# Chunked attention and a gated MLP on one core: the startup's loads and conversions in another order, half of the v loads on a second queue

## The chip, the core and the metric

The kernel runs on one core of a Trainium2 chip. The core has five engines with an instruction stream each: TensorE (PE in the profile), VectorE (DVE), ScalarE (ACT), GpSimd (POOL) and SyncE (SP, which only issues loads and stores here). An engine takes its instructions in order; what depends on another engine or on a load waits for a semaphore. The metric is the device time of one execution in microseconds, lower is better.

## The reference

Chunked attention over 4 batches, 8 heads, 768 positions and 64 channels, followed by a gated MLP (the code here leaves out the sizes and the plain loops):

```python
for c in range(nc):                      # 24 chunks of 32 queries
    k_ctx = k[:, :, max(0, 32*c - 16):min(S, 32*c + 40)]
    v_ctx = v[:, :, max(0, 32*c - 16):min(S, 32*c + 40)]
    k_full = concat(mem_k, k_ctx); v_full = concat(mem_v, v_ctx)     # 8 memory rows ahead
    a = softmax(scale * q_c @ k_full.T)
    out[:, :, c] = a @ v_full
x = out as (4, 768, 512)
h = relu(x @ w_in)                       # 512 -> 1024
u, v = halves of h
v_n = (v - mean(v)) / sqrt(var(v) + 1e-6)
v_s = w_spatial @ v_n + b_spatial        # over the 768 positions of a batch
result = (u * v_s) @ w_out               # 512 -> 512
```

All inputs are float32 but for w_in and w_out, which arrive as 64-bit floats.

## The kernel before, in words

**Attention.** A unit is four chunks, 128 queries, of all eight heads; a batch has six units (`UB`), a group of three units shares its loads of q and k (`GU`). For unit i TensorE makes the scores (`burst`, tile `sx`), VectorE takes the maximum and subtracts it, ScalarE takes the exp (`softmax`, tile `p`), TensorE transposes p (`flip`, tile `pt`), ScalarE copies that out (`pT`), TensorE multiplies with v (`f<-vmain,pT` in the first units, `sx<-v,pT` later), VectorE divides by the sum (`xs`), TensorE transposes (`xt`), ScalarE and VectorE write x as a high part and a low part. Unit i's product with v stands behind unit i+1's scores. With `PSUMS = 3` the sums of p of the first three units are made by TensorE (`f<-halves,pT`), later ones by VectorE (`den`).

**MLP.** Every product of the MLP is three products of the tile's high and low parts: high by high, low by high, high by low (`group`, lines 748 to 750, tile `f`, four buffers). I call three such products on one slice of 128 channels a chunk. `ffn_v` makes 128 rows of v in four chunks of 128x512, `ffn_u` u in four chunks of 128x384, `spatial` the product with w_spatial, `ffn_o` the last product.

**Weights.** w_in arrives as pairs of 32-bit words. `from_f64` loads a part (128 rows, the u half or the v half of the columns), and makes of it `win_h` and `win_l`: ScalarE scales the high words, VectorE shifts and sets the sign (two instructions, lines 922 and 923), ScalarE scales the low words ("rest"), GpSimd adds them, ScalarE casts the sum to the high part, GpSimd subtracts for the low part. w_spatial (`w_sp_part`) is cast and subtracted in the same way. All these loads share four buffers (`big`).

**v and the memory rows.** A unit's v has for two halves of the heads (r = 0, 1) 32 partitions of its own rows and 24 of the next chunk (the halo), and 8 of mem_v. In batch 0 the halo is copied on the chip (`shift_v`, line 486, on ScalarE or GpSimd), and mem_v is loaded for one chunk and spread by copies (`load_mem`, `copy_mem`, line 316).

**What sets the order.** All work is recorded by `op` in a plan (class `Plan`), with a rank, a length, what it reads and what it writes; `order` is a list scheduler that writes every engine's order out from that, and the program keeps to it. The table `FIRST` says which loads of batch 0 come in which order, with ranks for w_in's conversions. `heat` adds TensorE products of which nothing is used, as many as `HOT` says. Loads go out in SP's queue, except for mem_k and the first memory rows, which go out in ScalarE's; a load waits until at most 2 MB (`AHEAD`) are under way. Eight semaphores (DMAHW0 to DMAHW7) are given to the loads in turn as the program lists them; a load waits until the load eight places earlier has landed.

Of the kernel before, what the change touches and what calls it, by code (L numbers as in the profile page):

```python
# [25 lines left out]
FIRST = [("qk", 0, (0, 0), 1), ("mem", 0, "ACT", True), ("qk", 0, (1, 2), 2), ("w", 1, 1, 40.0, 3.0),  # L26
# [4 lines left out]
LANES = 8  # L31
CLOCK0 = 1.2
SHORT = 3.4133
HOT = (7, 4, 3, 7, 7, 0, 0)
# [3 lines left out]
PSUB = 0  # L38
XLOW = 0
PSUMS = 3  # L40
VACT = 6
VNORM = {"DVE": 0.6}
VLOW = {"DVE": 0.85}
KEYS = {"ACT": 0.42, "POOL": 0.43}
WLOW = {"POOL": 1.35}
SHIFT = {"POOL": 1.08, "ACT": 0.95}
SPREAD = {"ACT": 2.6, "POOL": 3.0}


# [27 lines left out]
class Plan:  # L77
# [12 lines left out]
    def op(self, eng, us, fn, r=(), w=(), rank=0.0, moves=0.0, tail=0.0, after=None, count=0):  # L90
        n = len(self.ops)
        deps, begun = set(), set()
# [18 lines left out]
        self.ops.append((eng, us, fn, deps, rank, moves, tail, held, begun, count))  # L111
        return n

    def order(self):
# [8 lines left out]
        free = {e: 0.75 if e in ("SP", "ACT") else 0.0 for e in ENGINES}  # L123
# [10 lines left out]
        while len(out) < len(ops):  # L134
            best = None
            for e, ns in waiting.items():
                pick = None
                for n in ns:
# [14 lines left out]
                    late = max(t, free[e])  # L153
                    if any(max(free[x], t) + y < late + either[n][e] for x, y in either[n].items() if x != e):
                        continue
                    c = (late, ops[n][4], n)
                    if pick is None or c < pick:
                        pick = c
# [3 lines left out]
            _, _, _, _, _, moves, tail, held, _, count = ops[n]  # L162
            us = either[n][e]
            if count:
                k, heat = clock.of(t), 0.5 if count in (128, 256) else 1.0
# [15 lines left out]
            free[e] = t + us  # L181
            if moves:
# [22 lines left out]
def tile_chunked_attention_gmlp(  # L205
# [67 lines left out]
    v2 = early.tile([P, T, GU * UC, D], F32, name="v2")  # L273
    ps = {name: pool(f"ps_{name}", bufs=sizes[name], space=PSUM) for name in ("f", "sx", "pt", "xt")}
# [3 lines left out]
    wsp_h = const.tile([P, ST, S], F32R, name="wsp_h")  # L278
    wsp_l3 = const.tile([P, ST - 3, S], F32R, name="wsp_l3")
# [20 lines left out]

    def heat(n, r=()):
        def go():
            if ("xt", "warm") not in t_:
                alloc("xt", "warm", [P, 512], F32, psum=True)
            for _ in range(n):
                nc.tensor.matmul(t_["xt", "warm"], minus, minus.unsqueeze(1).broadcast_to([P, T, P]), start=True, stop=True, skip_group_check=True)  # L306
        if n:
            op("PE", 0.233 * n, go, r=r, w=[("xt", "warm")], rank=99.0, tail=0.25, count=2 * n)

    def clear():  # L310
        for r in range(2):
            nc.vector.memset(vmain[r * D + CH:(r + 1) * D, :, 0], 0.0)
    op("DVE", 0.2, clear, w=["clear"], rank=-1.0)
# [7 lines left out]
    line, sent, held = {}, [], {}  # L321

    def load(dst, src_, w, rank, r=(), eng="SP", rows=P, us=0.45):
# [13 lines left out]
        def go():  # L337
            me["ins"] = e.dma_start(out=dst() if callable(dst) else dst, in_=src_).ins  # L338
            if before:
# [4 lines left out]
        speed *= {P: 1.0, CH: 0.75}.get(rows, 0.4)  # L344
        n = op(eng, us, go, r=[*r, *([("load", before["n"])] if before else [])], w=[*w, ("load", len(plan.ops))],
               rank=rank, moves=n / 1e6 / speed, after=line.get(eng))
        line[eng] = me["n"] = n
# [18 lines left out]

    def early_keys():
        return [key for key in plan.writer if isinstance(key, tuple) and key[0] == "early"]

    def wsp_l(s):  # L370
        return late("wsp_l0")[:, s] if s < 3 else wsp_l3[:, s - 3]
# [19 lines left out]
    def load_qk(g, units=(0, GU - 1), pieces=1):  # L391
        i = GU * g
        b, c0 = i // UB, (i % UB) * UC
# [585 lines left out]
    for i in range(UB):  # L979
        shift_v(i)  # L980
# [79 lines left out]
```

## Time and profile before

| What | Value |
|---|---|
| median of 3 runs | 398.62 us (397.97 to 399.00) |
| the profiled execution's own time | 398.16 us |
| its span, first to last instruction | 396.1 us |
| mean granted TensorE clock | 0.983 |
| TensorE busy | 383.8 us, 97% of the span |
| VectorE, ScalarE, GpSimd busy | 49%, 42%, 28% |

The profile is one execution. A row of the chain of waits is a start, a length and what ran or was waited for; a row of the timeline is a start, a length, the engine, the line, the operation, its tiles and shapes. A row of the stretches gives a window, its length, the busy time of PE, PEld (weight loads), DVE, ACT and POOL with the number of instructions, the granted TensorE clock, the mean share of the DMA engines that was busy and the GB/s moved. "SPq" and "ACTq" are the issue of loads, "issue" is time in which an engine waited for nothing that the profile shows. Line numbers are those of the kernel before.

### The profile page before, as it was taken

Reading aid. Unit: us, or ns where it says so; the run is one execution under the profiler, and the core shown is the slowest. Engines: PE = TensorE matmul, PEld = TensorE weight load, DVE = VectorE, ACT = ScalarE, POOL = GpSimd, SP = SyncE. Lnnn points to the kernel's source line nnn. Section 1 sums busy time; section 2 is a strip of 40 time slices with the busy share of each in tenths; the row PEclk is TensorE's granted clock in tenths of the full one; section 3 lists DMA queues with packets and bytes.
Section 4 is the critical chain, followed back from the end, with each engine's and each line's share of the span. In section 5 each row is a group of like instructions: output and inputs, shape, how many; then the busy total and the mean of one; then the engine's idle time right before and its main releaser. Section 6 shows DMA issues by size and latency. Waiting matters only on the chain.

```text
span 396.1 us, 11126 instructions
## 1 busy us (share of the span) xinstructions
PE 383.8 (97%) x4864; PEld 344.3 (87%) x4864; DVE 195.7 (49%) x392; ACT 165.1 (42%) x289; POOL 110.3 (28%) x119
## 2 busy tenths in 40 slices
PE   6797999999999999999999999999999999999996
PEld 4586898999899889889988988889989889899995
DVE  2746987895546447494662315383423233514040
ACT  6686986872524235344323223343221223321212
POOL 6497686285102101010220312010222210104031
PEclk9868999999999999999999999999999999999999
DMA  7999337972165582023746010000001010000202
GB/s 249 263 289 300 120 101 159 280 211 76 43 217 79 133 267 73 2 62 121 164 134 233 1 75 7 0 3 2 2 36 46 26 55 0 0 2 0 81 1 79
DMA packets 29216, 39.53 MB, mean 100 GB/s; under 512 B 5360, under 2 KB 23280, under 8 KB 29168
## 3 DMA queue, kind: packets, MB, share of 16 engines
q1 hardware_dynamic: 28864, 38.73, 32.7%
q8 instruction: 38, 0.62, 0.7%
q10 hardware_dynamic: 304, 0.10, 0.1%
q14 instruction: 10, 0.08, 0.1%
HBM read 32.52 MB, written 6.29 MB: 98 GB/s over the span
## 4 chain that ended last, share of the span: by engine, by line
PE 91%; DMA 7%; issue 1%; POOL 1%; SPq 0%; ACT 0%; POOLq 0%
PE f L748 26%; PE f L749 25%; PE f L750 25%; PE sx L546 8%; DMA vmain<-in_v_dram 3%; PE xt L699 3%; PE pt L682 3%; DMA big<-in_moe_w_in_dram 1%; PE f L546 1%; DMA k<-in_k_dram 1%; DMA vmain<-in_mem_v_dram 1%; PE xt L306 1%; POOL vmain L486 1%; SPq L338 0%; ACT st L890 0%
## 5 line engine op out<-in xcount | busy, mean ns | idle before, releaser
L858 POOL TENSOR_TENSOR st<-st,u 128x384 f32<-128x384 f32 x32 | 33.8, 1057 | 139.3 <-DVE st L854 106.0
L748 PE MATMUL f<-wsp_h,vn 128*128 128x384 f32 x192 | 66.4, 346 | 0.0
L749 PE MATMUL f<-wsp_h,vn 128*128 128x384 f32 x192 | 65.0, 339 | 0.0
L750 PE MATMUL f<-wsp_l,vn 128*128 128x384 f32 x192 | 64.5, 336 | 0.0
L786 POOL TENSOR_TENSOR rstd<-ve,mhalf 128x1 f32<-128x1 f32 x24 | 16.6, 691 | 102.2 <-DVE ve L782 102.2
L748 PE MATMUL f<-x,win_h 128*128 128x384 f32 x128 | 44.7, 350 | 0.0
L861 ACT CAST big<-st 128x384 fp32r<-128x384 f32 x32 | 16.4, 512 | 65.1 <-POOL st L858 65.1
L749 PE MATMUL f<-x,win_l 128*128 128x384 f32 x128 | 43.3, 338 | 0.0
L750 PE MATMUL f<-x,win_h 128*128 128x384 f32 x128 | 43.2, 337 | 0.0
L854 DVE TENSOR_TENSOR st<-f,bias 128x384 f32<-128x384 f32 x32 | 17.8, 556 | 51.3 <-PE f L750 51.3
L748 PE MATMUL f<-win_h,x 128*128 128x512 f32 x96 | 39.7, 413 | 0.0
L748 PE MATMUL f<-wout,big 128*128 128x512 f32 (+1 forms) x100 | 39.0, 390 | 0.0
L749 PE MATMUL f<-wout,big 128*128 128x512 f32 (+1 forms) x100 | 38.3, 383 | 0.0
L750 PE MATMUL f<-wout,big 128*128 128x512 f32 (+1 forms) x100 | 38.2, 382 | 0.0
L750 PE MATMUL f<-win_l,x 128*128 128x512 f32 x96 | 38.1, 397 | 0.0
L749 PE MATMUL f<-win_h,x 128*128 128x512 f32 x96 | 38.0, 396 | 0.0
L748 PEld LDWEIGHTS f<-wsp_h,vn 128*128 128x128 f32 x192 | 36.0, 188 | 1.4
L749 PEld LDWEIGHTS f<-wsp_h,vn 128*128 128x128 f32 x192 | 36.1, 188 | 0.8
L750 PEld LDWEIGHTS f<-wsp_l,vn 128*128 128x128 f32 x192 | 36.1, 188 | 0.0
L778 DVE BATCH_NORM_STATS2 stats<-st 128x6 f32<-128x512 f32 x24 | 16.6, 690 | 31.6 <-ACT st L774 31.6
L865 DVE TENSOR_TENSOR big<-st,big 128x384 fp32r<-128x384 f32 x32 | 20.6, 645 | 21.9 <-ACT big L861 21.6
L890 ACT COPY st<-f 128x512 f32<-128x512 f32 (+1 forms) x25 | 14.2, 571 | 31.3 <-PE f L750 30.9
(85 smaller groups left out, 704.8 us busy)
## 6 DMA issues: line engine op xcount, KB each, us to landing
out_dram<-st SPq DMA_DIRECT2D x23, 256.0 KB
k<-in_k_dram SPq DMA_DIRECT2D x7, 800.0 KB
q<-in_q_dram SPq DMA_DIRECT2D x7, 768.0 KB
vmain<-in_v_dram SPq DMA_DIRECT2D x36, 128.0 KB
big<-in_moe_w_in_dram SPq DMA_DIRECT2D x8, 512.0 KB
vmain<-in_v_dram SPq DMA_DIRECT2D x35, 96.0 KB
big<-in_moe_w_spatial_dram SPq DMA_DIRECT2D x6, 384.0 KB
big<-in_moe_w_out_dram SPq DMA_DIRECT2D x4, 512.0 KB
```

Of the source, the lines that this page charges most:

```text
L546: nc.tensor.matmul(o, w_, m, start=start, stop=True, skip_group_check=True)
L682: nc.tensor.transpose(a[:, t], p[:, t], ident)
L748: nc.tensor.matmul(o, lh, rh, start=(j == 0), stop=False)
L749: nc.tensor.matmul(o, ll, rh, start=False, stop=False)
L750: nc.tensor.matmul(o, lh, rl, start=False, stop=(j == len(pairs) - 1))
L778: nc.vector.bn_stats(stats, t_["st", s])
L786: nc.gpsimd.tensor_tensor(a, t_["ve", i], mhalf, op=ALU.pow)
L854: nc.vector.tensor_tensor(alloc("st", s_, [P, HT], F32), t_["f", n], bias[:, tok], op=ALU.add)
L858: nc.gpsimd.tensor_tensor(a, a, t_["u", i], op=ALU.mult)
L861: nc.scalar.copy(t_["g", i][:, 0, 0:HT], t_["st", s_])
L865: nc.vector.tensor_tensor(a[:, 1, 0:HT], t_["st", s_], a[:, 0, 0:HT].bitcast(F32), op=ALU.subtract)
L890: nc.scalar.copy(alloc("st", s_, [P, N], F32), t_["f", n])
```

## The change

- **v and mem_v in batch 0.** The r = 1 half of v goes out in ScalarE's queue (`TWO = 1`, `behind`). Unit 0 has its halo loaded, too; the others' is still copied. mem_v is no longer spread: `first_mem` loads it for three units at a time, eight loads of `8x12x64`, the first set in ScalarE's queue, the second in SP's. `copy_mem` and the clearing of v's rows go.
- **w_in.** The high part is cast from the high words alone, before the low words are added; the low part is the full sum less that. Scale and cast may run on GpSimd, the subtraction on VectorE.
- **u's half of w_in** is loaded into and converted in tiles of its own (`stage_w`, `stage_z`) in the place that w_spatial's parts take later; w_spatial's casts wait for the last low part of w_in.
- **Scores** of the first units use the two halves of one `sx` tile in turn (`HALVES`), so that the next scores need not wait for the last maximum and subtraction. The sums of p are all VectorE's (`PSUMS = 0`), and the addition of the small constant moves to ScalarE. The heating products go (`HOT = ()`).
- **The order.** The list scheduler counts a VectorE operation of a marked kind and any GpSimd operation as exclusive (`port`), has other lengths, and a table `ORDER` that adds to the ranks of some 75 operations, delays their choice, or fixes their engine.

Three places in which the order moves, for engines that wait or are waited for there. First ScalarE's order around unit 2's exp. Before (the first row is unit 2's exp, `pT` the copy of its transposed p, `x<-xt` x's high part, `k_158` the keys of units 3 to 5):

```order
L654 ACTIVATE p<-p 128x512 [waits DVE_49]
L931 CAST win_h<-st 128x512 [waits Pool_49]
L913 ACTIVATE st<-big 128x512
L316 COPY k_158<-k_158 128x16x24 [waits DMAHW5_49]
L705 CAST x<-xt 128x4x128 [waits PE_49]
L685 COPY pT<-pt 128x512 [waits PE_49,Activation_49]
L913 ACTIVATE st<-big 128x512 [waits DMAHW0_49,Pool_49]
```

And now, the same stretch with buffer numbers (`p_384` is unit 2's exp, `pT_460` its copy, `v2_94` the v of units 3 to 5, `x_361` the x of units 0 to 2):

```order
L981 ACTIVATE st_423<-big_356 128x512 [waits DMAHW2_49]
L987 ACTIVATE big_356<-big_356 128x512
L695 ACTIVATE p_384<-p_384 128x512 [waits DVE_49,Activation_49]
L375 DMA v2_94<-in_v_dram 32x4x768 [waits DMAHW4_49]
L353 CAST win_h_112<-st_423 128x512 [waits DVE_49]
L353 CAST win_h_112<-stage_z_99 128x512 [waits DVE_49]
L733 COPY pT_460<-pt_440 128x512 [waits PE_49,Activation_49]
L353 COPY k1_374<-k1_374 128x16x24
L704 ACTIVATE den_453<-den_453,tiny_119 128x8 [waits DVE_49]
L981 ACTIVATE stage_z_99<-stage_w_98 128x512 [waits DMAHW5_49]
L987 ACTIVATE stage_w_98<-stage_w_98 128x512
L538 COPY v2_94<-v2_94 24x4x192 [waits DMAHW6_49]
```

A load of v, with its wait for a semaphore of the loads, now stands between unit 2's exp and the copy of its transposed p.

Second, SP's order of loads from the second k on. Before (`big` takes parts of w_in):

```order
L338 DMA k1_158<-in_k_dram 128x4x400 [waits DMAHW3_49]
L338 DMA v2_94<-in_mem_v_dram 8x4x64 [waits DMAHW6_49]
L338 DMA v2_94<-in_mem_v_dram 8x4x64
L338 DMA big_410<-in_moe_w_in_dram 128x1024 [waits DMAHW4_49,DMAHW0_49,Pool_49]
L338 DMA big_554<-in_moe_w_in_dram 128x1024 [waits DMAHW1_49,Activation_49,Pool_49]
L338 DMA v2_94<-in_v_dram 32x4x256 [waits DMAHW5_49,DMAHW2_49]
```

And now (`stage_w` takes the u half of w_in):

```order
L375 DMA k1_374<-in_k_dram 128x4x400 [waits DMAHW4_49,DMAHW2_49]
L375 DMA stage_w_98<-in_moe_w_in_dram 128x1024 [waits DMAHW3_49]
L375 DMA v2_94<-in_v_dram 32x4x768 [waits DMAHW6_49]
L375 DMA v2_94<-in_v_dram 24x4x64
L375 DMA stage_w_98<-in_moe_w_in_dram 128x1024 [waits DMAHW4_49,DMAHW0_49]
L375 DMA v2_94<-in_mem_v_dram 8x12x64 [waits DMAHW1_49]
L375 DMA v2_94<-in_mem_v_dram 8x12x64 x3
L375 DMA v2_94<-in_mem_v_dram 8x12x64 [waits DMAHW5_49]
```

The eight loads of mem_v now stand behind the last part of w_in; in turn they take DMAHW1, 2, 3, 4 and on.

Third, TensorE's order around its first MLP products. Before (`sx<-k_158` are the scores of unit 3; a row `x32` is 32 instructions):

```order
L682 MATMUL pt<-ident,p 128x128 x4
L546 MATMUL sx<-k_158,q_297 32x64 x32
L546 MATMUL f<-halves,pT 128x2 x4
L546 MATMUL f<-vmain,pT 32x64 x32
L748 MATMUL f<-win_h,x 128x512
L749 MATMUL f<-win_h,x 128x512
L750 MATMUL f<-win_l,x 128x512
L699 MATMUL xt<-ident,xs 128x128 x4
```

And now (`sx<-k_374` are the scores of unit 3):

```order
L799 MATMUL f<-win_h,x 128x512 x2
L799 MATMUL f<-win_l,x 128x512
L730 MATMUL pt<-ident,p 128x128 x4
L799 MATMUL f<-win_h,x 128x512 x2
L799 MATMUL f<-win_l,x 128x512
L582 MATMUL f<-vmain,pT 32x64 x32
L582 MATMUL sx<-k_374,q_364 32x64 x32
L749 MATMUL xt<-ident,xs 128x128 x4
```

Two chunks of the first rows of v now stand ahead of unit 2's product with v and unit 3's scores, which stand behind the ScalarE copy of the first place.

The core of the diff (`...` marks what is left out; of the tables a line each):

```diff
-FIRST = [("qk", 0, (0, 0), 1), ("mem", 0, "ACT", True), ("qk", 0, (1, 2), 2), ("w", 1, 1, 40.0, 3.0),
+FIRST = [('w', 0, 1, 11.0, 14.0), ('qk', 0, (0, 0), 1), ('w', 1, 1, 14.0, 15.0), ('mem', 0, 3, 'ACT'),
...
-HOT = (7, 4, 3, 7, 7, 0, 0)
+HOT = ()
+ORDER = {
+    5: (-27, 0.8, ''), 6: (60, 1.5, ''), 8: (47, 0.4, ''), 9: (-57, 0, ''), 13: (-27, 0, 'POOL'), 17: (-17, 0.4, ''),
...
-PSUMS = 3
+PSUMS = 0
...
+    def wsp(name):
+        if name not in t_:
+            stage_scope.close()
+            a = pool("wsp", bufs=1, side="right")
+            t_["wsp_h"] = a.tile([P, ST, S], F32R, name="wsp_h")
...
         for r in range(2):
             g0 = (b * H + r) * NC + c0
             load(v4[r * D:r * D + CH], src(v, g0 * D, [[G * D, CH], [TS, T], [1, n * D]]),
-                 w=[vkey(j, r, 0) for j in range(i, i + units)], rank=10.0 * i, rows=CH)
+                 w=[vkey(j, r, 0) for j in range(i, i + units)], rank=10.0 * i, rows=P if two else CH,
+                 eng="ACT" if two and r else "SP", behind=two and r)
...
+    def first_mem(i, units, eng):
+        o, n = (i % NV) * UC, units * UC
+        for r in range(2):
+            for t in range(T):
+                load(v_tile(i)[(r + 1) * D - M:(r + 1) * D, t, o:o + n],
+                     src(mem_v, (2 * t + r) * M * D, [[D, M], [0, n], [1, D]]),
+                     w=[vkey(j, r, "m", t) for j in range(i, i + units)], rank=10.0 * i, eng=eng, rows=M, us=0.3)
...
-            op("ACT", 0.66, scale_, r=whole + ([] if gate is None else [("p", gate)]), w=[zk], rank=rank)
-            op("DVE", 1.55, shift, r=whole, w=[zk], rank=rank)
-            op("ACT", 0.66, rest, r=whole, w=[("big", big, "r")], rank=rank)
-            op("POOL", 1.4, add, r=[("big", big, "r")], w=[zk], rank=rank)
-            op("ACT", 0.6, high, r=[zk], w=[(*name, "h"), *over], rank=rank)
-            op(WLOW, 0, low, r=[zk, (*name, "h")], w=[(*name, "l"), *over], rank=rank)
+            op(SCALE, 0, scale_, r=whole + ([] if gate is None else [("p", gate)]), w=[zk], rank=rank)
+            op("DVE", 0.4, shift, w=[zk], rank=rank, port=True)
+            op("DVE", 0.62, sign, r=whole, w=[zk], rank=rank, port=True)
+            op(HIGH, 0, high, r=[zk], w=[(*name, "h"), *over], rank=rank)
+            op("ACT", 0.66, rest, r=whole, w=[(big[0], big, "r")], rank=rank + LATER)
+            op("POOL", 1.27, add, r=[(big[0], big, "r")], w=[zk], rank=rank + LATER)
+            op(WLOW, 0, low, r=[zk, (*name, "h")], w=[(*name, "l"), *over], rank=rank + LATER, port=True)
```

The lengths in these `op` lines are the scheduler's own assumptions.

More of the change, by code (lines that the diff above doesn't have):

```diff
@@ L38 @@
 PSUB = 0
+LATER = 1.0
+SCALE = {'ACT': 0.66, 'POOL': 0.75}
+HIGH = {'ACT': 0.6, 'POOL': 0.7}
+SINGLE = 0
+SINGLE_U = 0
+HALVES = 1
 XLOW = 0
-PSUMS = 3
+PSUMS = 0
 VACT = 6
[L42 to L47, printed above, removed]
+VNORM = {"DVE": 0.45}
+VLOW = {'DVE': 0.66}
+KEYS = {'ACT': 0.45, 'POOL': 0.48}
+WLOW = {'POOL': 1.27, 'DVE': 0.66}
+SHIFT = {'POOL': 1.03, 'ACT': 1.0}
 class Clock:
@@ L110, in op @@
         begun -= {*deps, n}
[L111 removed]
+        self.ops.append((eng, us, fn, deps, rank, moves, tail, held, begun, count, wait, port))
         return n
@@ L181, in order @@
             free[e] = t + us
+            if e == "POOL" or e == "DVE" and port:
+                free["port"] = t + us
             if moves:
@@ L299, in tile_chunked_attention_gmlp, with heat_f, go @@
     hot = [n for n in HOT]
+    def heat_f(n, r):
+        key_ = ("warm", len(plan.ops))
+        def go():
+            a = alloc("f", key_, [P, 512], F32, psum=True)
+            for _ in range(n):
+                nc.tensor.matmul(a, minus, minus.unsqueeze(1).broadcast_to([P, T, P]), start=True, stop=True,
+                                 skip_group_check=True)
+        if n:
+            op("PE", 0.233 * n, go, r=r, w=[("f", key_)], rank=99.0, tail=0.25, count=2 * n)
     def heat(n, r=()):
@@ L319, in src, with load @@
         return bass.AP(tensor=t.tensor, offset=offset, ap=ap)
-    line, sent, held = {}, [], {}
-    def load(dst, src_, w, rank, r=(), eng="SP", rows=P, us=0.45):
+    line, sent, held, whole_v = {}, [], {}, set()
+    def load(dst, src_, w, rank, r=(), eng="SP", rows=P, us=0.45, behind=False):
         e = {"SP": nc.sync, "ACT": nc.scalar}[eng]
@@ L454, in load_v @@
         last = (i + units) % GU == 0
+        if halo:
+            whole_v.update(range(i, i + units))
         TS = 2 * NC * D
+        two = b == 0 and TWO
         for r in range(2):
@@ L467, in part @@
                 load(dst, src_, w=[vkey(j, r, s) for j in (range(i, i + units) if halo else [i + units - 1])],
-                     rank=10.0 * i, rows=HALO)
+                     rank=10.0 * i, rows=2 * HALO if two else HALO, eng="ACT" if two and r else "SP", behind=two and r)
             o = v4[r * D + CH:r * D + CH + HALO, :, (n - m) * D:]
@@ L540, in prep, with score_key @@
         if i % GU == 0:
-            op("POOL", 0.3, mem, r=["memT"], w=[key("k", g) + ("mem",)], rank=rank)
+            op("POOL", 0.3, mem, r=["memT"], w=[key("k", g) + ("mem",)], rank=rank, after=t_["began", g])
         op(KEYS if i < UB else {"ACT": 0.42}, 0, keys, r=qk_keys(i, "k"), w=[key("k", g) + ("next",)], rank=rank)
+    def score_key(i):
+        if i <= SPLIT and HALVES:
+            return ("sx", "first", i % 2)
+        return ("sx", (i, "sp" if i > SPLIT else "s"), 0)
     def burst(i, rank):
```

221 lines of the change are left out of this document (124 added, 97 removed), and 14 rows, old and new, of tables (FIRST, ORDER).

## The prediction

> **What bounds the kernel now.** I read the page first, then TensorE's waits, then the chain of waits in order of time. The page:
>
> ```profile
> span 396.1 us, 11126 instructions
> PE 383.8 (97%) x4864; PEld 344.3 (87%) x4864; DVE 195.7 (49%) x392; ACT 165.1 (42%) x289; POOL 110.3 (28%) x119
> ```
>
> TensorE is busy for 383.8 of 396.1 us. The two longest of its six waits:
>
> ```profile
> PE xt L306 <- ACT minus L297: 3.0, 1, 3.0
> PE f L546 <- issue: 2.0, 1, 2.0
> ```
>
> The first is for the table of the heating products, at the very start; the second stands in the chain of waits, in order of time, just ahead of the end of the first stage:
>
> ```profile
> 31.25 2.01 issue
> 33.26 0.93 PE f L546 x41
> 34.19 0.72 PE f L748
> 34.91 0.43 PE f L749
> ...
> 37.29 0.44 PE pt L682 x4
> ...
> 41.18 0.23 PE f L749
> 41.42 0.24 PE f L750
> 41.65 1.69 PE sx L546 x103
> 43.34 0.43 PE f L748
> ```
>
> The first FFN product runs at 34.19 us, and from there TensorE hardly stops. So the kernel is a startup and then one long block of TensorE work, and the change is worth what it does to the startup. The products at 34.91 take 0.43 us, those at 41 us 0.23: TensorE had paused until 33.26, and some 3.4 us later it runs at full speed.
>
> I need a place that means the same in both programs. It is the end of unit 3's product with v, the second half of the row at 41.65, which ends at 43.34. Before it TensorE's order has units 0 to 3 and seven chunks of three products 128x512 (one row `f<-win_h`, one more, one `f<-win_l`); the changed order has the same units and the same seven chunks before that product. I call this place P. What follows P is the same amount of TensorE work, so the change of the time is the change of P, unless TensorE stops later.
>
> **When the loads land.** The stretches of the trace, 5 us each; the last columns are clock, DMA share and GB/s:
>
> ```profile
> 0.00:5.00 5.00, 2.04 (x5) 1.65 (x6) 0.81 (x8) 1.68 (x3) 1.92 (x10) 1.00 0.59 169
> 5.00:10.00 5.00, 4.36 (x72) 2.60 (x70) 1.55 (x3) 4.84 (x3) 4.88 (x3) 1.00 0.98 332
> 10.00:15.00 5.00, 3.98 (x74) 3.15 (x75) 3.25 (x6) 4.41 (x8) 1.25 (x3) 0.76 0.93 301
> 15.00:20.00 5.00, 3.20 (x74) 2.49 (x73) 4.63 (x6) 2.16 (x3) 3.05 (x3) 0.84 0.93 218
> 20.00:25.00 5.00, 4.66 (x76) 3.94 (x77) 1.83 (x6) 4.94 (x9) 4.31 (x6) 0.50 0.95 301
> 25.00:30.00 5.00, 5.00 (x150) 4.29 (x149) 2.84 (x3) 3.85 (x9) 4.53 (x4) 0.88 0.88 279
> 30.00:35.00 5.00, 2.99 (x74) 2.56 (x75) 2.95 (x10) 2.35 (x5) 3.98 (x4) 0.80 0.97 265
> ```
>
> Summed up, 0.85 MB have moved at 5 us, 2.51 at 10, 4.01 at 15, 5.10 at 20, 6.61 at 25, 8.00 at 30 and 9.33 at 35. The DMA engines are nearly full, so a load's place in this sum gives its time. A test: in the program before, the second k load (units 3 to 5) is complete at 6.77 MB (sizes by the tiles), which the sum puts at 25.6 us. The six loads of v behind it wait for it:
>
> ```profile
> 26.71 2.61 SPq L338 DMA_DIRECT2D v<-in_v_dram  x6
> ```
>
> They go out at 26.71. Landing, then, is the sum's time plus 1.1 us.
>
> **The change part by part.** *The loads' order and the second queue.* A load takes one of eight semaphores in turn, and waits until the load eight places earlier has landed. Half of the v loads now stand in ScalarE's queue, and such a wait there holds all ScalarE's work behind it. The place that counts is `v2<-in_v_dram 32x4x768`, right behind unit 2's exp: the 45th load, on DMAHW4. The load before it on that semaphore is the 37th, the fourth of eight `v2<-in_mem_v_dram 8x12x64`, and these stand in SP's queue behind the last part of w_in, which itself waits for the second k. So ScalarE cannot cast the last high parts, nor copy unit 2's pT, until the fourth mem_v row set has landed. TensorE stands behind that copy: unit 2's product with v, and everything after it, is in order.
>
> When is that? Loads up to the second k: six parts of w_in 3.15 MB, q and k of units 0 to 2 1.61, their v 1.03, mem_k and mem_v 0.26, the next q and k 1.61: 7.65 MB. Behind it: two parts of w_in 1.05, half of v 0.42, four mem_v 0.10: 9.22 MB. The sum puts 9.22 MB at 30 + 1.22/0.265 = 34.6, and landing at 35.7 us. I call it H.
>
> Two things move H. The v loads fill 32 partitions and run at 218 GB/s in 15 to 20 us against 301 beside it; if two queues cure that, 1.03 MB gain 1.3 us. The mem_v loads, of short rows, are dearer than their bytes:
>
> ```profile
> 122.09 3.48 DMA vmain<-in_mem_v_dram
> ```
>
> That fourth of a set landed after 3.48 us; less 1.1, four take 2.4, or 0.6 each, where by bytes one takes 0.09. Twelve stand ahead of H, so this costs 0 (if others move beside them) to 6 us. I take both as cancelling, and keep 31.3 to 38.7 for H: the low end is 332 GB/s from 5 us on (5 + 8.37/0.332 + 1.1), the high end half of the 6 us.
>
> The Trainium skill's page "DMA: Bandwidth & Descriptors", section "Rules for kernel authors", says that spreading loads over issuing engines adds no bandwidth, since all of them run on the same 16 DMA engines; only issue time is saved. By that rule the 1.3 us are not gained and H is at most that much later; the row at 15 to 20 us, with a DMA share of 0.93 at 218 GB/s, does not decide it.
>
> *From H to P.* Durations on ScalarE and TensorE, from the timeline:
>
> ```profile
> 39.00 2.12 ACT L486 COPY v<-v 24x1024 f32<-24x1024 f32 x2
> ...
> 42.25 0.83 ACT L486 COPY v<-v 24x768 f32<-24x768 f32 x1
> 43.10 1.14 ACT L931 CAST win_h<-st 128x512 fp32r<-128x512 f32 x2
> ...
> 44.82 0.50 ACT L316 COPY k<-k 128x384 f32<-128x384 f32 x1
> 45.36 0.63 ACT L654 ACTIVATE p<-p 128x512 f32<-128x512 f32 x1
> ...
> 46.64 0.56 ACT L705 CAST x<-xt 128x512 fp32r<-128x512 f32 x1
> 47.23 0.59 ACT L685 COPY pT<-pt 128x512 f32<-128x512 f32 x1
> 47.71 0.68 ACT L913 ACTIVATE st<-big 128x512 f32<-128x512 f32 x1
> 48.28 0.71 ACT L918 ACTIVATE big<-big 128x512 uint32<-128x512 uint32 x1
> ```
>
> ```profile
> 27.23 0.86 PE L546 MATMUL f<-vmain,pT 64*32 64x64 f32 x64
> ```
>
> ScalarE: the issue (0.3), two casts (1.14), unit 2's pT (0.6) end at H + 2.05. Then the key copy 0.5, the denominator's addition (a new instruction on 8 columns, 0.2 taken, 0 to 0.5), a scale and a rest of w_in 1.3, a v copy 0.83, x's cast 0.55, two v copies 2.1, the next cast 0.55 and unit 3's exp 0.6: H + 8.6. TensorE meanwhile: product with v and unit 3's scores 0.86 each, a transpose 0.5, two chunks with three products cold at 0.43 and three warm at 0.23, a transpose 0.45, two chunks 1.4: H + 8.1. It then waits for that exp. Unit 3's transpose 0.44 brings H + 9.0; a chunk (0.7) and the scores of unit 4 (0.8) run while ScalarE copies v once more (1.04) and then pT (0.6); the product with v (0.8) ends at P = H + 11.2. VectorE's work on that stretch, unit 3's maximum and subtraction, unit 2's norm and the low half of x, fits beside it, since ScalarE is later.
>
> So P moves from 43.3 to 35.7 + 11.2 = 46.9, by +3.6 us.
>
> *The rest.* The heating products and the products that summed p go: they fill gaps of TensorE that end by other things, so I give nothing for them; without heat three FFN products are cold, which is in the sum. w_in's high part from the high words alone takes a GpSimd add out of the way to `win_h`; it lets the first two chunks run before H, and they are among the seven. GpSimd's new scale and cast of 128x512 have no row; the nearest, copies and adds there, run from 0.5 to 1.3 us, and they lie in the time in which ScalarE is held. u's half in w_spatial's place needs w_spatial's casts to wait for the last low part. The 2.01 us at 31.25 ("issue") lie before P; if they come again, P is 2 us later, and I give 0 as TensorE's order now has a long pause ahead of its bursts.
>
> Against the profiled execution's own 398.16 us this gives 401.8; that execution is 0.46 us under the median of the three runs (398.62). I say 401.7.
>
> **The rivals.** *The hold does not bind (faster).* If the fourth mem_v lands before ScalarE comes to it, or does not stand behind w_in's last part, unit 3's scores start when its k has landed: 7.65 MB, 28.7 + 1.1, and a key copy of 0.5, at 30.3 us instead of H + 2.9 = 38.6. P would be 8.3 us earlier, and the time 393.5. For it: ScalarE's other needs by then (w_in's fourth v part, at 6.04 MB) have landed by 24.2. Against it: the order of both queues and the eight semaphores, and a full DMA. It decides from H under 31 us on.
>
> *Loads are quick (no change).* With H at 31.3 to 33.5, the hold costs what the earlier v and w_in gain: 397.3 to 399.5. The windows of 332 and 301 GB/s speak for it, those of 218 and 265, both with v loads in them, against.
>
> *GpSimd becomes late (slower still).* Behind H it has a copy of keys, one of v, a scale, a cast, four adds, a reciprocal root and two subtractions:
>
> ```profile
> 30.16 1.29 POOL L928 TENSOR_TENSOR st<-st,big 128x512 uint32<-128x512 uint32 x1 [0.63 <-DVE st L923]
> 31.39 0.29 POOL L539 COPY k<-memT 128x128 f32<-128x128 f32 x1
> 31.64 2.49 POOL L935 TENSOR_TENSOR win_l<-st,win_h 128x512 fp32r<-128x512 f32 x2
> ```
>
> Six of these at 1.27 are 7.6, the others some 3.5; with the waits for VectorE the last low part comes at about H + 18.5. TensorE wants it some 9 us behind P, at H + 20. If GpSimd loses 4 us more, the time is 404.5 or above.
>
> **How the numbers follow.** The hold decides, with H from 33.6 to 38.5: 0.62, time 399.6 to 404.6. Quick loads: 0.14. The hold does not bind: 0.17. GpSimd late on top: 0.07. The likeliest is the first, 401.7. A measurement of this kernel tells about 0.3%, 1.2 us, from no change; so faster is the case without a hold, 0.17, and 0.02 of the quick loads, together 0.19; within it are 0.12 of the quick loads and 0.01 of the forecast's lower edge, 0.13; slower is the rest, 0.61 and 0.07, together 0.68. For the range I leave out the last rival and most of the hold-free case: 396.5 to 404.8.
>
> **What would show it.** The changed profile should show ScalarE without work from about 27 us until the fourth `v2<-in_mem_v` lands near 35.7, then its casts; TensorE's `f<-vmain,pT` of unit 2 some 2 us later; the product that ends P near 46.9; and nothing new after it. If unit 2's product with v comes at 30 us, the hold is not there. If P is near 46.9 but the end is not 3.6 later, TensorE's later work was not the same. If the v loads still show about 218 GB/s, the second queue gave nothing.

## The result and the profile after

The changed kernel takes 411.75 us (median of 4 runs, 409.25 to 414.33) against 398.81 us of the kernel before beside it (4 runs, 397.97 to 400.36): a ratio of 1.032, with a 95% interval of 1.0242 to 1.0399. It is slower, as forecast, but by 12.9 us and not by 3.1. The profiled execution took 414.33 us, the longest of the four, with a span of 412.5 us and a mean clock of 0.975. Of the runs below, the times are medians of the executions in the chip's faster state, which leaves out two of e1 and one each of g1, h1 and h5.

The page of the changed kernel:

```profile
span 412.5 us, 11015 instructions
PE 372.2 (90%) x4812; PEld 335.1 (81%) x4812; DVE 190.6 (46%) x378; ACT 160.3 (39%) x300; POOL 106.4 (26%) x117
```

TensorE is busy for 11.6 us less (the heat and the summing products are gone) in a span that is 16.4 us longer, so 28 us more of it are idle. Its longest waits (us in total, times, longest):

```profile
PE sx L582 <- ACT k L353: 13.4, 3, 11.7
PE f L582 <- ACT pT L733: 11.9, 3, 10.1
PE pt L730 <- ACT p L695: 7.1, 1, 7.1
```

All three name ScalarE. The 11.7 us are the start of the program, before the first scores (they ran at 11.73 us; in the kernel before at 6.25). ScalarE was held there behind its own loads of the first mem_v set, and once more behind two of its loads of v:

```profile
11.12 0.51 ACT L353 COPY k<-k 128x384 f32<-128x384 f32 x1 [8.25 <-DMA vmain<-in_mem_v_dram]
19.30 0.63 ACT L695 ACTIVATE p<-p 128x512 f32<-128x512 f32 x1 [5.98 <-DMA vmain<-in_v_dram]
```

The 10.1 us are the longest stop once TensorE has begun its MLP products. What ScalarE did there, from its timeline:

```profile
29.83 0.65 ACT L695 ACTIVATE p<-p 128x512 f32<-128x512 f32 x1
41.06 0.32 ACTq L375 DMA_DIRECT2D v<-in_v_dram  x1
41.42 0.62 ACT L353 CAST win_h<-st 128x512 fp32r<-128x512 f32 x1 [10.94 <-DMA v<-in_mem_v_dram]
41.95 0.61 ACT L353 CAST win_h<-stage_z 128x512 fp32r<-128x512 f32 x1
42.47 0.58 ACT L733 COPY pT<-pt 128x512 f32<-128x512 f32 x1
```

After unit 2's exp it issues nothing until 41.06 us: the load of v2 is held, two casts and unit 2's pT are queued behind it, and TensorE behind that pT. This is the hold of the prediction, instruction by instruction, but H, the end of the wait, is 41.06 us where 35.7 was forecast. The chain of waits carries it to P (start, length):

```profile
27.32 6.79 DMA k<-in_k_dram
...
35.66 5.38 DMA v<-in_mem_v_dram
...
42.56 0.49 ACT pT L733
43.09 1.24 PE f L582 x64
...
46.31 2.56 PE f L799 x6
...
53.66 0.43 PE sx L582 x25
54.09 3.52 PE f L799 x15
```

P is 54.09, against 43.34 before and 46.9 forecast. There is also a stop that was not forecast, 50 us later, on TensorE's timeline:

```profile
103.11 0.85 PE L582 MATMUL sx<-k,q 64*32 64x64 f32 x64 [1.28 <-ACT k L353]
...
106.52 0.21 PE L582 MATMUL sx<-vmain,pT 64*32 64x64 f32 x1 [1.82 <-issue]
```

From P to the end the span has 412.5 - 54.1 = 358.4 us, and before it had 396.1 - 43.3 = 352.8. So of the 16.4 us of these two executions 10.7 stand ahead of P and 5.6 behind it.

### The profile page after: what moved, and what is told of

The parts are those of the page before. It is cut to its first block, busy times and chain, and to the rows that moved or that the text cites. A ratio compares the mean times of both kernels' runs of the same rounds, so it can differ in the third digit from the quotient of the medians.

```text
span 412.5 us, 11015 instructions
## 1 busy us (share of the span) xinstructions
PE 372.2 (90%) x4812; PEld 335.1 (81%) x4812; DVE 190.6 (46%) x378; ACT 160.3 (39%) x300; POOL 106.4 (26%) x117
## 4 chain that ended last, share of the span: by engine, by line
PE 77%; DMA 19%; SPq 1%; issue 1%; ACT 1%; ACTq 0%
PE f L799 66%; PE sx L582 7%; DMA k<-in_k_dram 6%; DMA vmain<-in_v_dram 3%; DMA big<-in_moe_w_in_dram 3%; PE xt L749 2%; PE pt L730 2%; DMA big<-in_moe_w_out_dram 2%; DMA q<-in_q_dram 2%; DMA v<-in_mem_v_dram 1%; DMA vmain<-in_mem_v_dram 1%; SPq L375 1%; PE f L582 0%; ACT k L353 0%; ACT win_h L353 0%
## 5 line engine op out<-in xcount | busy, mean ns | idle before, releaser
L799 PE MATMUL f<-wsp_h,vn 128*128 128x384 f32 x384 | 101.3, 345 | 0.0
L799 PE MATMUL f<-x,win_h 128*128 128x384 f32 x256 | 73.3, 342 | 0.0
L799 PE MATMUL f<-wout,big 128*128 128x512 f32 (+1 forms) x300 | 71.8, 383 | 0.0
L799 PEld LDWEIGHTS f<-wout,big 128*128 128x128 f32 x300 | 54.1, 188 | 8.8
L799 PEld LDWEIGHTS f<-x,win_h 128*128 128x128 f32 x256 | 47.1, 188 | 1.4
L799 PE MATMUL f<-x,win_l 128*128 128x384 f32 x128 | 43.3, 338 | 0.0
L842 POOL TENSOR_TENSOR rstd<-ve,mhalf 128x1 f32<-128x1 f32 x24 | 16.4, 684 | 98.1 <-DVE ve L838 98.1
L918 ACT CAST big<-st 128x384 fp32r<-128x384 f32 x32 | 16.4, 512 | 64.9 <-POOL st L915 64.9
L799 PEld LDWEIGHTS f<-win_h,x 128*128 128x128 f32 x192 | 35.1, 193 | 5.8 <-issue 0.2
L582 PE MATMUL sx<-k,q 64*32 64x64 f32 x1536 | 21.7, 235 | 14.2 <-ACT k L353 13.4
L582 PEld LDWEIGHTS sx<-k,q 64*32 64x32 f32 x1536 | 17.6, 110 | 20.8 <-issue 19.7
L695 ACT ACTIVATE p<-p 128x512 f32<-128x512 f32 x24 | 15.1, 631 | 34.0 <-DVE p L680 28.0
L759 DVE TENSOR_TENSOR x<-xt,x 128x512 fp32r<-128x512 f32 x24 | 16.4, 683 | 25.3 <-ACT x L755 25.3
```

The costliest lines, as they stand in the source:

```text
L582: nc.tensor.matmul(o, w_, m, start=start, stop=True, skip_group_check=True)
L695: nc.scalar.activation(p3, p3, AF.Exp, scale=scale)
L759: nc.vector.tensor_tensor(x[:, 1, :, o:o + UT], t_["xt", j], x[:, 0, :, o:o + UT].bitcast(F32), op=ALU.subtract)
L799: nc.tensor.matmul(o, ll if x == 1 else lh, rl if x == 2 else rh, start=x == j == 0, stop=j == len(pairs) - 1 and x == (single[-1] if sing ...
L842: nc.gpsimd.tensor_tensor(a, t_["ve", i], mhalf, op=ALU.pow)
L918: nc.scalar.copy(t_["g", i][:, 0, 0:HT], t_["st", s_])
```

## The experiments

Two theories at the start. The hold (the prediction's own, later called H): ScalarE behind one load of v2. Against it, that the loads as a whole are late, whatever is held (later called A). The runs are named by the labels of their expectations; "left out" in an expectation says which part of the result a run does not compute.

### First four: undo one part, and let the planner order the rest

`e1_v2_sp`: only units 0 to 2 keep the second queue.

```diff
-        two = b == 0 and TWO
+        two = b == 0 and TWO and i < GU
```

> Only the r = 1 half of the v of units 3 to 5 goes back to SyncE's queue; ScalarE then has no load between unit 2's exp and the copy of its pT. P is the end of unit 3's product with v, at 43.3 us before the change and 54.0 after it. Hold theory (ScalarE waits 10.9 us for the fourth mem_v load): unit 2's pT follows its exp within 3 us, so TensorE goes on at about 34 us; unit 3's scores then wait for their k, which landed at 34.1; P at 43.5 to 45. If the stop of TensorE at 102 to 107 us only follows from P, it goes as well and the time is 398 to 400; if it is the later order's own, 403 to 405. Rival (the loads are late whichever engine issues them): ScalarE or TensorE finds another late load in the same place, P stays over 49 and the time over 407.

`e2_one_queue`: no second queue.

```diff
-TWO = 1
+TWO = 0
```

> All v loads of batch 0 in SyncE's queue, as before the change; all else as changed (the scheduler rewrites the order with that). Hold theory: as with the run above no load holds ScalarE behind unit 2's exp, P at 43.5 to 46. On the second queue itself: if it brings bandwidth, the second k lands later than the 34.1 us of the change, by the 1.3 us that the prediction gave it or more; if it brings none, the second k lands at 34 us or earlier. Rival (loads late): P over 49.

`e4_mem_early`: the second set of mem_v loads ahead of w_in's last part.

```diff
-('w', 3, 0, 42.0, 5.0), ('mem', 3, 3, 'SP'),
+('mem', 3, 3, 'SP'), ('w', 3, 0, 42.0, 5.0),
```

> The eight mem_v loads of units 3 to 5 stand ahead of the last part of w_in, not behind it; ScalarE still issues the v half and still waits for a semaphore, now that of the third mem_v load. Hold theory: ScalarE goes on when that load has landed, some 3 us earlier than the 41.0 us (without 0.52 MB ahead of it and one mem_v load fewer): 37 to 38.5, P at 50 to 51.5, time 2.5 to 4 us under the changed kernel's. Rival (loads late, the place of the wait does not matter): ScalarE goes on at 41 as before, P within 1 us of 54.

`e3_no_table`: the table of offsets is not used.

```diff
-        if n in ORDER:
+        if n in ():
```

> The table ORDER is not used; everything else is as changed, and the scheduler writes the order by its own rules. Its order still has two loads of v in ScalarE's queue behind unit 2's exp, waiting for the fourth and fifth mem_v loads, so by the hold theory it is as late: ScalarE goes on at 41 to 42, P at 52 to 56, time 409 to 416. Rival (the searched table is what costs the time): P under 47, time under 404.

Measured: e1 409.99 and 408.37 us (ratio 1.0264, 1.0204 to 1.0325), e2 417.02 (1.0473, 1.0415 to 1.053), e4 416.26 (1.0473, 1.0408 to 1.0539), e3 416.55 (1.0448, 1.0397 to 1.05). The table is worth about 5 us, then, with intervals that just touch; but none of the edits gave anything back that can be told from the changed kernel. What the expectations said of P under the hold did come true: in e4 the held load went out at 38.50 us and P was 50.8, and in e1 the hold is gone, the same seven chunks stand ahead of P, and P ends at 44.1 us, next to the 43.3 of the kernel before. The times did not follow: the span less P is 363.3 in e4 and 364.0 in e1, against 358.4 in the changed kernel. TensorE's timeline in e1, from P on:

```profile
43.24 0.85 PE L582 MATMUL sx<-v,pT 64*32 64x64 f32 x64
44.02 0.74 PE L799 MATMUL f<-win_h,x 128*128 128x512 f32 x2
44.60 0.40 PE L799 MATMUL f<-win_l,x 128*128 128x512 f32 x1
50.44 1.11 PE L730 MATMUL pt<-ident,p 128*128 128x128 f32 x4 [5.45 <-ACT p L695]
```

One chunk after P it stops for 5.45 us, for an exp. The chain of waits of that run says what was ahead of the exp: the last part of w_in and its conversion.

```profile
32.77 8.26 DMA stage_w<-in_moe_w_in_dram
...
45.11 1.75 DVE win_l L1007
```

Such a stop is not in the changed kernel: there TensorE has five chunks of v and one of u between P and that transpose, in e1 one chunk. The planner orders everything anew after any edit. The times of these four runs weigh an edit and a new order together, and cannot tell the theories apart.

### The next four: loads, heat and conversion, still ordered anew

With the hold gone and nothing gained, the lateness of loads (theory A) looked the better theory.

`e5_no_mem`: the sixteen loads of mem_v out.

```diff
     def first_mem(i, units, eng):
+        for m in range(2 * T):
+            if i == 0 and m < 2:
+                e, o = (nc.vector, vmain) if m == 0 else (nc.gpsimd, v2)
+                op("DVE" if m == 0 else "POOL", 3.3, lambda e=e, o=o: e.memset(o, 0.0), w=[("clear", m)], rank=-1.0)
```

> The changed kernel without the sixteen loads of mem_v rows (8x12x64 each) of batch 0: both v tiles are set to zero at the start instead, so the values of batch 0's memory rows are left out of its product with v. Theory A (the small loads make everything behind them late: with the first set in the queues 15 to 20 us moved 179 GB/s and with the second 35 to 40 us moved 163, where 25 to 30 moved 311, and ScalarE stood 8.2 and 10.9 us behind such a load): the second k load lands at 30 or earlier instead of 34.1, ScalarE has no wait over 5 us for a load of mem_v, and the time is 399 to 404. Rival B (the order of the instructions, which puts w_in ahead of q, k and v, sets the start whatever the loads do): first scores still near 11, and 408 to 412, as with the halves of v2 on SyncE's queue (412.6).

`e6_before_mem`: the changed kernel's `first_mem` in the kernel before.

```diff
-("mem", 0, "ACT", True)
+("mem", 0, 3, "ACT")
-("copy",)
+("mem", 3, 3, "SP")
```

> The kernel before, with the sixteen 8x12x64 loads of the changed kernel in place of its own six small loads and four spreading copies on ScalarE and GpSimd. Theory A: 404 to 411, most of the change's loss, although four copies are saved. Rival B: within 2 us of the kernel before, 397 to 401, since the order of w_in, q, k and v is untouched. Anything from 401 to 404 gives the loads a part only.

`e7_before_cold`: no heat in the kernel before.

```diff
-HOT = (7, 4, 3, 7, 7, 0, 0)
+HOT = ()
```

> The kernel before without its 31 heating products (HOT empty), nothing else. Theory A and rival B both leave the time within 1 us, 398 to 400, since these products stood in TensorE's waits for loads. Rival C (the clock: without heat early, the stretch of half clock falls on work; in the changed kernel the clock was 0.67 and 0.55 from 30 to 50 us, in the one before 0.80, 0.69 and 0.83 from 10 to 40): 401 or more, with a clock under 0.8 in a stretch where TensorE works.

`e8_before_high`: the changed conversion in the kernel before.

```diff
-            op("ACT", 0.6, high, r=[zk], w=[(*name, "h"), *over], rank=rank)
+            op(HIGH, 0, high, r=[zk], w=[(*name, "h"), *over], rank=rank)
+            op("ACT", 0.66, rest, r=whole, w=[("big", big, "r")], rank=rank + LATER)
+            op("POOL", 1.27, add, r=[("big", big, "r")], w=[zk], rank=rank + LATER)
```

> The kernel before with the changed conversion of w_in alone: high part from the high words, scale on ScalarE or GpSimd, the low part's steps later; no second queue, no half in w_spatial's place, own order of loads. Theory A: no loss, 396 to 400. Rival D (the conversion's eight longer steps on GpSimd, 1.5 us for a scale where ScalarE took 0.69, and the low parts behind them hold TensorE): 401 or more, with waits of TensorE for win_l or for GpSimd.

Measured: e5 427.63 us (1.0708, 1.0659 to 1.0757), e6 400.79 (1.0042, 1.0007 to 1.0076), e7 407.51 (1.0189, 1.0121 to 1.0257), e8 403.60 (1.0137, 1.0058 to 1.0217). Taking sixteen loads out made the kernel 16 us slower, which neither theory has. In e5 the longest wait group of TensorE:

```profile
PE pt L730 <- ACT p L695: 21.8, 8, 6.2
```

TensorE's first FFN product runs at 55.88 us in e5, in the changed kernel at 29.96, although the second k goes out earlier (23.69 us against 27.32). That the order, not the loads, made e5 slow is what the next runs test. e6 stands as a first hint against theory A as I had put it: in the kernel before, in place of six small loads and four copies and with a new order, sixteen such loads cost 0.4%.

### With the order kept

From here on the order that the planner had made for the kernel is written out as a list, and an edit changes only its own instructions; on every engine the others stand row for row as they did. In the expectations Q stands for the second queue as the cause, O for the order of the instructions, C for the clock, and R for the halves of v of units 0 to 2 in ScalarE's queue.

```diff
+KEPT = [
...
+]
     def order(self):
+        self.on = dict(map(tuple, KEPT))
+        return [n for n, _ in KEPT]
```

`g1_kept_no_mem` takes the sixteen loads out as e5 did, `g2_kept_one_queue` gives the halves of v to SP, `g3_kept_both` does both, `g4_before_kept_cold` takes the heat out of the kernel before.

```diff
-        e = {"SP": nc.sync, "ACT": nc.scalar}[eng]
+        e = nc.sync if behind else {"SP": nc.sync, "ACT": nc.scalar}[eng]
```

> The changed kernel with its order of instructions kept row for row on every engine, and only the sixteen loads of mem_v rows of batch 0 taken out (both v tiles set to zero at the start, so those rows' values are left out of the product with v). In the run without them at 427.6 the planner had put everything in another order, so that run did not weigh the loads. Theory A (the small loads are late and make the rest late): 400 to 405, second k landing at 31 or earlier, no hold of ScalarE over 3 us between 30 and 42. Theory Q (it is the halves of v on ScalarE's queue that lower the rate and hold ScalarE): 408 to 412. Theory O (order and holds elsewhere): 408 to 412 as well.

> The changed kernel, order kept row for row, but the six loads of the second halves of v that ScalarE issues stand in SyncE's queue at the same place. Theory Q: 401 to 407, with 250 GB/s or more moved from 15 to 20 us (179 in the changed kernel) and ScalarE not held at 35 to 41. Theory A: 408 to 413, the second k no earlier than 33. Theory O: within 3 us of the changed kernel either way.

> The changed kernel, order kept row for row, without the sixteen loads of mem_v (those rows' values left out, as above) and with all halves of v in SyncE's queue. If the loads' lateness, of whatever cause, is the whole loss (A and Q together), the time is 396 to 401 and the stop near 103 us is gone. If the order of the instructions itself costs time (theory O), it stays at 404 or more with landings as early as the plan's (second k at 27).

> The kernel before, order kept row for row, without its 31 heating products. In the run at 407.5 the planner, whose clock goes by the heat, had moved other instructions too. Theory C (heat is worth what that run lost): 404 or more. If the loss there was the new order: 397 to 400, and heat is worth nothing measurable.

Measured: g1 402.20 us (1.0072, 1.0037 to 1.0107), g2 404.15 (1.0116, 1.0072 to 1.016), g3 402.39 (1.0075, 1.0037 to 1.0114), g4 398.88 (0.9993, 0.996 to 1.0025). The same edit that gave 427.6 with a new order (e5) gives 402.2 with the old one, and that of e2, at 417.0, gives 404.2. Either edit alone brings back much of the loss, 9.5 us and 7.6, and both together no more than one: this points to a common cause, which needs the small loads and the second queue at once. Theories A and Q each had the other edit at 408 or more, and both are wrong in that. Heat is worth nothing that shows in the kernel before, and the 8.7 us of e7 were its new order.

Stretches of 5 us of g1, and then one of g2 (the last columns are clock, DMA share and GB/s):

```profile
0.00:5.00 5.00, 0.00 (x0) 0.00 (x0) 2.83 (x7) 1.79 (x3) 3.39 (x8) 1.00 0.57 152
5.00:10.00 5.00, 1.17 (x64) 0.96 (x64) 1.95 (x4) 1.20 (x2) 3.00 (x4) 1.00 1.08 289
10.00:15.00 5.00, 1.53 (x6) 0.89 (x6) 3.04 (x6) 2.61 (x5) 3.08 (x3) 1.00 1.09 282
15.00:20.00 5.00, 3.53 (x150) 2.82 (x151) 2.95 (x6) 3.27 (x5) 2.81 (x4) 1.00 1.05 340
20.00:25.00 5.00, 2.21 (x79) 1.65 (x80) 3.52 (x7) 3.95 (x8) 3.93 (x5) 0.74 0.91 287
```

```profile
15.00:20.00 5.00, 3.28 (x132) 2.64 (x132) 3.85 (x9) 3.79 (x8) 1.62 (x3) 1.00 1.09 277
```

The changed kernel's own:

```profile
0.00:5.00 5.00, 0.00 (x0) 0.00 (x0) 0.27 (x6) 1.68 (x3) 0.79 (x7) 1.00 0.51 133
5.00:10.00 5.00, 0.00 (x0) 0.00 (x0) 1.12 (x2) 0.00 (x0) 2.38 (x3) 1.00 1.05 287
10.00:15.00 5.00, 1.17 (x64) 0.96 (x64) 1.55 (x3) 1.16 (x2) 1.52 (x2) 1.00 1.10 236
15.00:20.00 5.00, 0.01 (x1) 0.01 (x1) 1.75 (x4) 0.69 (x2) 1.23 (x1) 1.00 1.13 179
20.00:25.00 5.00, 4.13 (x136) 3.33 (x136) 3.10 (x7) 4.83 (x8) 3.53 (x4) 1.00 0.93 271
25.00:30.00 5.00, 3.08 (x135) 2.21 (x133) 4.08 (x8) 4.86 (x11) 3.92 (x5) 0.85 0.93 311
30.00:35.00 5.00, 2.98 (x13) 2.10 (x10) 3.88 (x9) 0.48 (x1) 0.91 (x2) 0.81 0.92 278
35.00:40.00 5.00, 0.00 (x0) 0.00 (x0) 0.00 (x0) 0.00 (x0) 0.00 (x0) 0.54 0.83 163
40.00:45.00 5.00, 1.91 (x128) 1.91 (x128) 1.52 (x4) 3.55 (x8) 1.29 (x1) 0.50 0.63 140
45.00:50.00 5.00, 5.00 (x38) 4.00 (x21) 3.88 (x9) 3.87 (x6) 4.08 (x6) 0.60 1.05 405
```

The loads of mem_v move few bytes and take the DMA engines' time: from 15 to 20 us, with them and two queues 179 GB/s at a share over 1, with them and one queue 277, without them 340; and from 35 to 40 us 163 in the stretch of the second set, in which no engine works (238 in g1). The Trainium skill's page "DMA: Bandwidth & Descriptors", section "Rules for kernel authors", has the rule that many small transfers are to be made one large one, as under 64 KB the overhead is most of what one pays; these are 24 KB each, and the rows agree.

### The hold by itself, the later stop, and two tries on the kernel before

`h1_kept_v2_sp` moves only the two loads of v2's second half (operations 82 and 84 of the plan; the edit of e1, order kept) to SP's queue, `h2_kept_no_mem3` takes out only the second set of mem_v, `h4_kept_k_early` is g2 with the third q and k (counted from 0: those of units 9 to 11) ahead of twelve v loads, and `i1_kept_all` is g3 with that, too. `h3_before_v_one` and `h5_before_two` are the kernel before, order kept: h3 with v of units 0 to 2 ahead of the fourth part of w_in, h5 with only the second half of that v in ScalarE's queue. In h3, h4 and i1 a moved load no longer waits for a load that now stands behind it.

```diff
-        e = {"SP": nc.sync, "ACT": nc.scalar}[eng]
+        e = nc.sync if len(plan.ops) in (82, 84) else {"SP": nc.sync, "ACT": nc.scalar}[eng]
```

> The changed kernel, order kept row for row, with only the two loads of the second half of v2 (32x4x768 and its 24x4x64) moved from ScalarE's queue to the same place in SyncE's. Theory H (the prediction's hold: ScalarE stands behind that one load until the fourth mem_v load has landed, with the exponential's successors queued behind it, and the lateness of the loads matters through that): 403 to 406, all that the six halves in SyncE's queue gave back (404.2). Theory R (the four halves of v of units 0 to 2 on the second queue, with ScalarE held behind them at 13 to 19 us and 179 GB/s moved, are the cost): 408 to 412.

> The changed kernel, order kept row for row, without the second set of eight mem_v loads alone (v2 set to zero at the start; the values of the memory rows of units 3 to 5 are left out). Theory H: that set is what the held load waits for, so most of the 9.5 us comes back, 402 to 405, though the first set still holds ScalarE to 11. Theory R, or a cost that lies in the first set: 407 to 411, with the second k still landing after 33.

> The changed kernel, order kept row for row, all halves of v in SyncE's queue (404.2 that way), and the loads of the third q and k moved ahead of the twelve loads of v that stand before them in SyncE's queue. The 5.4 us that were left over the kernel before: if the later stop (TensorE without work at 90 to 95 us, behind a k that lands at 93 with six us of load behind twelve v loads) is half of it or more, the time is 400 to 402 and the stop is gone. If what is left lies in the start (first scores 11.7 instead of 6.3), it stays at 403 to 406.

> Not the change but what its runs point to: the kernel before, order kept, with the four loads of v of units 0 to 2 one place earlier in SyncE's queue, ahead of the fourth load of w_in instead of behind it. They land 1.5 us earlier, and with 7.84 us of the chain of the kernel before being that load, the time should be 397 to 398; if the w_in part that becomes later holds TensorE at 33 to 36 instead, 399 or more.

> The changed kernel, order kept row for row but for one pair of loads: all halves of v in SyncE's queue, no mem_v loads of batch 0 (those rows' values left out of the product with v), and the third q and k ahead of the twelve loads of v. If late loads at the start and at the later stop are all of the loss, this is 397 to 400, level with the kernel before. If 401 or more, some 2 us or more of the loss lies in the changed order itself or in work that no load explains.

> The change's first named part alone: the kernel before, order kept row for row, with the second half of v of units 0 to 2 (32x4x768 and 24x4x64) issued by ScalarE in the same place of the program instead of by SyncE. If a second queue brings these loads in earlier, 397 to 398.5, for 7.84 us of the chain of the kernel before are this load. If a second queue adds nothing but a hold of ScalarE behind the load eight places earlier (the prediction's mechanism), 400 or more, with ScalarE waiting for a load at 12 to 17 us; between the two it is worth nothing either way.

```diff
-        e = {"SP": nc.sync, "ACT": nc.scalar}[eng]
+        e = nc.scalar if len(plan.ops) in (39, 41) else {"SP": nc.sync, "ACT": nc.scalar}[eng]
```

Measured, all runs of the changed kernel with its order kept in one table. P and span are of the one profiled execution, which lies up to 3.2 us from the median of its row; each ratio is to the kernel before beside it, with medians from 398.1 to 399.2:

| run | us | ratio to before (95%) | P | span less P |
|---|---|---|---|---|
| the changed kernel | 411.75 | 1.032 (1.0242 to 1.0399) | 54.1 | 358.4 |
| h1, without the hold at v2 | 405.14 | 1.0158 (1.0078 to 1.0238) | 46.8 | 355.4 |
| h2, no second set | 404.38 | 1.0122 (1.004 to 1.0204) | 49.2 | 356.5 |
| g2, one queue | 404.15 | 1.0116 (1.0072 to 1.016) | 46.5 | 355.9 |
| h4, g2 and k early | 403.43 | 1.0103 (1.0062 to 1.0145) | 45.6 | 353.4 |
| g1, no mem_v loads | 402.20 | 1.0072 (1.0037 to 1.0107) | 43.2 | 353.9 |
| g3, g1 and g2 | 402.39 | 1.0075 (1.0037 to 1.0114) | 43.5 | 354.1 |
| i1, g3 and k early | 400.32 | 1.0049 (1.0016 to 1.0082) | 43.8 | 353.5 |
| the kernel before | 398.81 | | 43.3 | 352.8 |

h1 moves two loads, and half of the loss is gone, with intervals of the ratio that just do not meet: theory H. Its row of the product that ends P, and, from g1, the held load's issue:

```profile
45.66 1.09 PE L771 MATMUL sx<-v,pT 64*32 64x64 f32 x64
```

```profile
29.50 0.36 ACTq L564 DMA_DIRECT2D v<-in_v_dram  x1
```

g1 leaves the held load on ScalarE's queue; with no mem_v loads, the load eight places earlier on its semaphore is another one, it goes out at 29.50 us, and the hold is short. Between h1 and g1 lie 0.9 points, with intervals that overlap, and 3.6 us of P. In h1 the two earlier waits of ScalarE are still there, 8.4 us and 5.0, and unit 0's exp runs at 18.36 us, in g1 at 10.95; so I put this part down to the lateness of the loads at the start, which is argued and not shown by a run of its own. The later stop shrinks with P, though not in step: TensorE's idle time from 90 to 110 us is 3.8 us in the changed kernel, 3.7 in h2, 2.9 in g2, 2.4 in h1, 1.5 in g1 and 0.8 in h4, where k is moved. The stretch from 90 to 100 us of g2 and then of h4:

```profile
90.00:100.00 10.00, 7.07 (x159) 6.49 (x158) 6.99 (x10) 2.92 (x6) 6.49 (x5) 1.00 0.35 115
```

```profile
90.00:100.00 10.00, 9.21 (x174) 8.62 (x173) 7.88 (x12) 4.28 (x9) 6.49 (x5) 1.00 0.42 115
```

TensorE has 2.1 us more of work in that stretch, and the profiled spans differ by 3.4 us; the medians differ by 0.7, with intervals that overlap, so what k early is worth is not settled. i1 was to show whether anything is left when the loads are on time: 0.49% is, some 2 us. Behind P it still has a stop of 1.75 us without a named cause (the kernel before has one of 2.01, ahead of P):

```profile
93.73 0.51 PE L988 MATMUL f<-wsp_h,vn 128*128 128x384 f32 x2 [1.75 <-issue]
```

h3 401.22 us (1.0053, 1.0011 to 1.0094): earlier v loads made the kernel before a little slower, against the expectation; TensorE then waited 3.1 us for a copy of v on GpSimd. h5 397.71 us (0.9995, 0.9957 to 1.0032): the second queue alone, for the v of units 0 to 2, is worth nothing either way. No run is faster than the kernel before by more than its interval.

## Why the prediction came out wrong, step by step

- **The mechanism** was right: one load of v2 on ScalarE's queue waits for the fourth mem_v load of the second set, and ScalarE, TensorE and all the rest with it. h1 shows its price with that load (and the halo's behind it) alone moved: 411.75 to 405.14, 6.6 us, and 7.3 us in P. Two earlier waits of the same kind, until 11.12 and 19.30 us, were not in the prediction; by them unit 2's exp came at 29.83 and not near 27, but the hold to 41.06 ended later than what they delayed.
- **The step that failed** is "I take both as cancelling", of the mem_v loads' cost and the second queue's gain. It put the cost of these loads at nothing net, and with that H at 35.7; H came 5.4 us later. There was no gain to set against the cost: the second queue gained nothing by itself (h5), and with the mem_v loads beside it the rate fell to 179 GB/s. Summed up as the prediction did it, but with the changed kernel's own rows, 5.53 MB have moved at 25 us (6.61 in the kernel before, 6.75 in g1), and 9.22 MB at 39.6. With 1.1 us for the landing that is 40.7, and H was 41.06: the sum of bytes and the landing time were sound, the curve was borrowed from a program without these sixteen loads. At 25 us g3, which has neither them nor the second queue, has moved 6.70 MB, g2 with them and one queue 6.26: the loads make the stream late, and with two queues more so. The high end of H, 38.7, gave them half of 6 us; the second set alone took 6.5 us from its first issue to the landing of its fourth load (34.58 to 41.06), with the last part of w_in and half of v2 under way beside it.
- **From H to P**: 13.0 us (41.06 to 54.09), where 11.2 were given. The order was as written; the clock was not. After 10 us without work TensorE ran at 0.50 and 0.60 from 40 to 50 us: both chunks at 46.31 took 2.56 us for six products, 0.43 each, where I had let three of them be warm, and the same holds for the scores and the transpose ahead of them. TensorE worked from 43.09 to 53.3 us without a stop, and unit 3's exp (49.96) was done when TensorE came to it, where I had TensorE wait for it.
- **"Nothing new after it"** failed: 5.6 us more behind P. 3.8 of them are TensorE's idle time from 90 to 110 us, and 1.7 are the products of the next 5 us, of which three take 0.96 us instead of 0.52 at first. I had followed one chain to P and let the stream of loads behind it be. Had it had slack, the scores at 103.11 would not have waited: the chain of waits there leads to the k of the next batch (issued at 96.07, in the kernel before at 85.16), which stands in SP's queue behind twelve loads of v and all that was late.
- **The heat given at nothing** was right as far as the kernel before shows it (g4, 0.9993), and GpSimd, the last rival, was no bound: TensorE has no wait for it in the changed kernel's profile. The rival without a hold, 393.5, was wrong twice: the hold was there, and without it (h1) the kernel stays 1.6% above the one before.
- **A slip in the last sum:** 398.16 and 3.6 give 401.8 for the profiled execution, and so 402.2 for the median, not 401.7. It changes nothing here.
- **Not settled:** the 0.5% that i1 leaves, and the changed conversion of w_in. e8 has it at 1.4% but with a new order, and as it changes the instructions themselves, the order could not be kept. Nor do the runs tell what TensorE's stops are for which the profile names no cause ("issue"): 2.3 us in the kernel before and 2.7 in the changed one, but 5.0 in h1, 9.2 in g2, 4.2 in g1, 6.5 in g3 and 3.1 in i1. So part of what these runs still lose may lie there and not in the loads.

## What to carry to other kernels

A load issued from an engine that also computes is a wait in that engine's order: before moving one there, find the load whose semaphore it takes over, and price that one's landing, with every load ahead of it, small ones by their time and not their bytes. When a planner writes the order, an edit and its new order are two changes; keep the order as a list and edit under it, or the measurement is of the order (402.2 against 427.6 us for the same edit). And a startup that ends late can be paid for again where the same stream of loads is next waited for (5.6 us here).

## What the runs showed of the hardware that I had not expected

- A stop costs twice. In the changed kernel 64 scores took 1.17 us at 44.09, after the hold, and 0.86 at 51.93. The Trainium skill's page "TensorE: Matmul & The Clock Gate", section "Part 1: The HAM clock gate (the "warmup" mystery)", says that the array's clock is halved after a pause and released by sustained work; the trace agrees, with 0.50 and 0.60 granted from 40 to 50 us and 1.00 from 50 on.
- The clock column does not show this everywhere. It reads 1.00 from 10 to 15 us in the changed kernel, yet the same 64 scores took 1.17 us there, as long as at half clock:

```profile
11.73 1.17 PE L582 MATMUL sx<-k,q 64*32 64x64 f32 x64 [11.73 <-ACT k L353]
...
51.93 0.86 PE L582 MATMUL sx<-k,q 64*32 64x64 f32 x64
```

- Two queues move little more than one. The two stretches of h5 in which the v loads are under way, 301 and 218 GB/s in the kernel before:

```profile
10.00:15.00 5.00, 4.12 (x75) 3.30 (x76) 2.84 (x5) 4.17 (x8) 0.91 (x2) 0.74 0.94 311
15.00:20.00 5.00, 2.78 (x72) 2.02 (x70) 4.83 (x6) 2.81 (x5) 3.29 (x3) 0.84 0.94 230
```

The time is the same (ratio 0.9995), as by the rule of the Trainium skill's page "DMA: Bandwidth & Descriptors", section "Rules for kernel authors", that the prediction cites.
